# Taking a row's 32nd largest score as the eighth of one MAX8, one pipeline step later

## The chip, the cores and the metric

The kernel runs on one core of a Trainium2 chip. The metric is the device time of one execution in microseconds (us): 872.44 us as the median of three runs of the kernel before (871.95 to 874.28).

The engines are called by the profile's names: PE (TensorE matmuls), PEld (its weight loads), DVE (VectorE), ACT (ScalarE), POOL (GpSimd) and SP (SyncE, which here only issues DMAs).

## The reference

For 4 batches, 8 heads, 576 tokens and 64 channels a head, the program computes a sparse attention, a gated convolution block and a mixing block behind it. Only the attention's top-k is touched here:

```python
scores = scale * np.matmul(q, k.transpose(0, 1, 3, 2))
kth = np.partition(scores, -top_k, axis=-1)[..., -top_k:-top_k + 1]   # top_k = 32
mask = scores >= kth
scores = np.where(mask, scores, -1000000000.0)
scores = scores - np.max(scores, axis=-1, keepdims=True)
attn = np.exp(scores)
attn = attn / (np.sum(attn, axis=-1, keepdims=True) + 1e-09)
```

The attention's output goes through the gated block (`_moe_ref`) and the mixing block (`_moe2_ref`), which are matrix products with 512x512 and 576x576 weights.

## The kernel before, in words

The scores come as 144 tiles of 128 rows by 576 columns. The main loop runs over pipeline steps; in step i each stage works on another tile, and the list `STEP` (for the first 72 steps `SOON`) sets the order of the stages within a step. The orders of DVE and ACT are exactly the order in which the program is written (`FIXED`); PE, POOL and SP are ordered by a planner, by priorities that follow the written order and by when it expects inputs to be ready.

A tile j passes these stages:

- Step j, `pick`: six MAX8 (L573), each over 96 columns, leave 48 candidates a row.
- Step j+1, still `pick`: three MAX8 (L577) and two MATCH_REPLACE8 (L579) over the 48 candidates give the row's 24 largest candidates, `tops`; the 24th is the bound t.
- Step j+1, `count` (ACT, L585): n is the sign of t against each score, +1 where the score is below t and -1 elsewhere, and its sum over the row goes to `acc`. So `acc` = 576 - 2c, where c is how many scores are not below t. c is 24 unless one block of 96 columns held more than eight of the row's largest.
- Step j+2, `below` (POOL, L593): y = score times n, so all scores at or above t become negative.
- Step j+3, `rest` (DVE, L598): MAX8 over y gives the eight largest scores below t. The tile y has a single buffer, so `below` of the next tile waits for this MAX8.
- Once for each group of three tiles, `select` puts three DVE operations into the list `apart`: L611 compares `acc` with eight constants (`counts`), L613 multiplies the outcome by the eight values, L614 adds them up. What is left is the one value that is the row's 32nd, in `thrs`. `mask_between` issues them one at a time around the mask of a step: L611 before the mask, L613 and L614 behind it, each behind an operation of the weights' conversion if there is one.
- Step j+5, `expo` (ACT), and step j+6, `mask` (DVE, L656): the score is compared with the threshold and multiplied by the exponential, in place.

Behind these stand the transposes, the products with v, the convolution, and as `jobs` the matmuls of the two blocks, of which each step takes a portion by planned cost. GpSimd also does subtractions that split numbers into a high and a low part (L244 for heads, L403 for matrices), the convolution's first sum (L796), joins converted weights (L342), negates maxima (L603), and prepares sums (L700).

`check` looks once, behind the last tile, whether any threshold is not to be trusted; then the whole work would be done again in a slower way (`safe`), which the inputs here don't need.

Of the kernel before, what the change touches and what calls it, by code (L numbers as in the profile page):

```python
# [92 lines left out]
def mixer(ctx, tc, qT, kT, vt, w_val, conv_t, w_out, w_theta, w_tok, w_ch, out, flag):  # L93
    nc = tc.nc
    safe = flag is None
    P = 128
    B, S, DM = vt.shape
# [5 lines left out]
    G = 3  # L103
    NSUB = 6
    SUB = S // NSUB
    K = 32
    KC = 24
# [3 lines left out]
    CUT = 2 * P  # L111
    COLS = ((0, CUT), (CUT, S))
    LAG = G + FLAG

    cp = ctx.enter_context(tc.tile_pool(name="cp", bufs=1))
    io = ctx.enter_context(tc.tile_pool(name="io", bufs=1))
    sp = ctx.enter_context(tc.tile_pool(name="sp", bufs=1))
    wk = ctx.enter_context(tc.tile_pool(name="wk", bufs=1))
# [34 lines left out]
    N = len(seq)  # L153
# [10 lines left out]
    make_identity(nc, ident)  # L164
    ones = cp.tile([P, 1], F32, name="ones")
    nc.gpsimd.memset(ones, 1.0)
    counts = cp.tile([P, G, K - KC], F32, name="counts")
    for i in range(K - KC):
        nc.gpsimd.memset(counts[:, :, i : i + 1], S - 2.0 * (K - 1 - i))
    trig_bias = cp.tile([P, 1], F32, name="trig_bias")  # L170
    nc.gpsimd.memset(trig_bias[:64], math.pi / 2)
    nc.gpsimd.memset(trig_bias[64:], 0.0)
# [3 lines left out]
    nc.gpsimd.memset(magic, MAGIC)  # L176

    awake = cp.tile([P, 1], F32, name="awake")
    said = cp.tile([1, 2], F32, name="said")
    thrs = cp.tile([P, N], F32, name="thrs")  # L180
    least = cp.tile([P, N, 2], F32, name="least")
    taken, lacking = set(), {}
    raws, heads, there, ready = {}, {}, set(), set()
    s_tiles, s_psum, groups, xT, gate, W, ms = {}, {}, {}, {}, {}, {}, {}
    owed = [0.0]
    jobs, later, mid, extras, chains, flowing, fill, apart = [], [], [], [], [], [], [], []

    evicted = [None]
    last = {}

    def tabled(out, src, func, **more):

        ins = nc.scalar.activation(out, src, func, **more).ins  # L193
        table = func == AF.Sin
        if (not table) in last and TABLED:
            tc.add_manual_dep(ins, last[not table].name, mybir.DependencyInfo(
                mybir.DependencyClass.NoSync, mybir.DependencyReason.DATA), reason="one table at a time")
        last[table] = ins

    def run(fs):  # L200
        for f in fs:
            f()
# [342 lines left out]
    def scores_out(i):  # L545
        banks = s_psum.pop(i)
        if i < N:
            st = sp.tile([P, S], F32, tag="s", name=f"s_{i}", bufs=LAG + TO + AHEAD)
            for (lo, hi), (bank, _) in zip(COLS, banks):
                evicted[0] = nc.scalar.activation(st[:, lo:hi], bank[:, : hi - lo], AF.Copy, scale=0.125).ins  # L550
            s_tiles[i] = st
        for _, follow in banks:
            run(follow)

    def group(i):
        g, k = divmod(i, G)
        if g not in groups:
            d = {}
            for nm, shape in (("cand", [P, G, 8 * NSUB]), ("tops", [P, G, K]), ("acc", [P, G]),
                              ("eq", [P, G, K - KC])):  # L560
# [20 lines left out]
    def count(i):  # L581

        d, k = group(i)
        n = wk.tile([P, S], BF16, tag="n", name=f"n_{i}")
        nc.scalar.activation(n, s_tiles[i], AF.Sign, bias=d["tops"][:, k, KC - 1 : KC], scale=-(1.0 + 2.0 ** -22),  # L585
                             accum_out=d["acc"][:, k : k + 1])
        d["n", k] = n

    def below(i):

        d, k = group(i)
        y = wk.tile([P, S], F32, tag="y", name=f"y_{i}")
        nc.gpsimd.tensor_tensor(y, s_tiles[i], d.pop(("n", k)), ALU.mult)  # L593
        d["y", k] = y

    def rest(i):
        d, k = group(i)
        nc.vector.max(d["tops"][:, k, KC:K], d.pop(("y", k)))  # L598

    def nmax(g):  # L600

        d = groups[g]
        nc.gpsimd.tensor_scalar(least[:, g * G : g * G + G, :], d["tops"][:, :, 0 : KC : KC - 1], -1.0, None, ALU.mult)  # L603

    def select(g):

        if safe:
            return one_by_one(g)
        d = groups[g]
        tops, acc = d["tops"], d["acc"]  # L610
        apart.append(lambda: nc.vector.tensor_tensor(  # L611
            d["eq"], counts, acc.unsqueeze(2).broadcast_to([P, G, K - KC]), ALU.is_equal))
        apart.append(lambda: nc.vector.tensor_tensor(d["eq"], d["eq"], tops[:, :, KC:], ALU.mult))  # L613
        apart.append(lambda: nc.vector.tensor_reduce(thrs[:, g * G : g * G + G], d["eq"], mybir.AxisListType.X, ALU.add))  # L614

    def one_by_one(g):

        d = groups[g]
        spare = wk.tile([P, S], F32, tag="ct", name=f"spare_{g}")
        for k in range(G):  # L620
            src = s_tiles[g * G + k]
            for r in range(K // 8):
# [5 lines left out]
            nc.vector.tensor_copy(thrs[:, g * G + k : g * G + k + 1], d["tops"][:, k, K - 1 : K])  # L628
        nmax(g)

    def check():

        bad = cp.tile([P, 2], F32, name="bad")
        worse = wk.tile([P, S], F32, tag="ct", name="worse")[:, :N]
        nc.vector.tensor_scalar(worse, thrs, 2.0 ** -100, None, ALU.is_le)
        nc.vector.tensor_reduce(bad[:, 0:1], worse, mybir.AxisListType.X, ALU.add)
        nc.vector.tensor_scalar(worse, least[:, :, 1], -2.0 ** -100, None, ALU.is_ge)
        nc.vector.tensor_reduce(bad[:, 1:2], worse, mybir.AxisListType.X, ALU.add)

        def on_pe(spare):  # L640
            nc.tensor.matmul(spare[:1, :2], ones, bad, start=True, stop=True)
            return lambda: nc.scalar.activation(said, spare[:1, :2], AF.Copy, accum_out=flag)
        extras.append((2, on_pe))

    def expo(i):
        e = seq[i]
        e.exp = wk.tile([P, S], F32, tag="e", name=f"e_{i}", bufs=2)
        tabled(e.exp, s_tiles[i], AF.Exp, bias=least[:, i, 0:1], scale=1.0)

    def mask(i):  # L650
        e = seq[i]
        part = e.part
        if e is part["tiles"][0]:
            part["sums"] = wk.tile([P, 5], F32, tag="sums", name=f"sums_{e.u}_{e.x}", bufs=3)
        p = s_tiles[i]
        nc.vector.scalar_tensor_tensor(p, p, thrs[:, i : i + 1], e.exp, ALU.is_ge, ALU.mult,  # L656
                                       accum_out=part["sums"][:, e.slot : e.slot + 1])

    def turn(i):
# [559 lines left out]
    for k, part in enumerate(order):  # L1219
# [27 lines left out]
    def mask_between(i):  # L1247

        for x in range(3):
            for fs in (fill, apart):  # L1250
                if fs:
                    fs.pop(0)()
            if x == 0:
                inside(i, mask)

# [10 lines left out]
    def inside(i, f):  # L1266
        if 0 <= i < N:
            f(i)
# [18 lines left out]
    def by_group(i, f):  # L1287
        if i % G == 0:
            inside(i, lambda i: f(i // G))
# [4 lines left out]
    def work_1(i):  # L1294
# [3 lines left out]
    DO = {  # L1298
        "count": lambda i: None if safe else inside(i - 1, count),
        "expo": lambda i: inside(i - LAG + 1, expo),  # L1300
        "select": lambda i: by_group(i - G - 2, select),
        "nmax": lambda i: None if safe else by_group(i - G - 1, nmax),
        "check": lambda i: None if safe or i != N + G else check(),
        "mask": lambda i: mask_between(i - LAG),
# [2 lines left out]
        "chains": lambda i: follow_up(),  # L1307
        "convert": convert,
        "pick": lambda i: i <= N and (by_group(i, group_of) if safe else pick(i)),
        "below": lambda i: None if safe else inside(i - 2, below),  # L1310
        "scores_out": lambda i: i + AHEAD - 1 in s_psum and scores_out(i + AHEAD - 1),
        "turn_out": lambda i: inside(i - LAG - TO - 1, turn_out),
        "rest": lambda i: None if safe else inside(i - 3, rest),
        "later": lambda i: run_later(),
        "turn": lambda i: inside(i - LAG - TO, turn),
        "work_1": work_1,
# [60 lines left out]
```

## Time and profile before

| | |
|---|---|
| median of three runs | 872.44 us |
| the profiled execution | 878.3 us |
| its span, first to last instruction | 876.5 us |
| mean granted TensorE clock | 0.932 |
| DVE busy | 725.9 us, 83% of the span |
| PE busy | 757.3 us, 86% |
| ACT busy | 652.3 us, 74% |
| POOL busy | 409.2 us, 47% |

The busy time of an engine is the union of its instructions, so two that overlap in the pipeline count once. A line such as "L613 DVE ... x48 | 16.9, 353 | 0.0" tells the line of the program, the engine, the operation, what it writes and reads, how often, the busy microseconds, the mean nanoseconds of one, and the idle time of the engine before them with what ended it. In a timeline the first number is the start, the second the duration, and brackets hold idle time before it.

### The profile page before, as it was taken

Reading aid. Unit: us, or ns where it says so; the run is one execution under the profiler, and the core shown is the slowest. Engines: PE = TensorE matmul, PEld = TensorE weight load, DVE = VectorE, ACT = ScalarE, POOL = GpSimd, SP = SyncE. Lnnn points to the kernel's source line nnn. Section 1 sums busy time; section 2 is a strip of 40 time slices with the busy share of each in tenths; the row PEclk is TensorE's granted clock in tenths of the full one; section 3 lists DMA queues with packets and bytes.
Section 4 is the critical chain, followed back from the end, with each engine's and each line's share of the span. In section 5 each row is a group of like instructions: output and inputs, shape, how many; then the busy total and the mean of one; then the engine's idle time right before and its main releaser. Section 6 shows DMA issues by size and latency. Waiting matters only on the chain.

```text
span 876.5 us, 15920 instructions
## 1 busy us (share of the span) xinstructions
PE 757.3 (86%) x4526; PEld 575.6 (66%) x4526; DVE 725.9 (83%) x2952; ACT 652.3 (74%) x1591; POOL 409.2 (47%) x435
## 2 busy tenths in 40 slices
PE   4477876947879689989798999999998999999995
PEld 2344554624556358676678577769697776699895
DVE  5999998879999778989999999899988697444522
ACT  5787896878979587687878898798987895445611
POOL 4655555344555324354758634445677233003700
PEclk9996788966899979999899999999999999999998
DMA  5665555613433124324735552132755110042001
GB/s 148 169 183 166 143 141 152 174 48 92 131 92 93 43 67 128 94 55 114 225 112 185 191 163 61 46 94 58 216 135 154 44 67 15 1 155 93 3 1 58
DMA packets 73601, 94.35 MB, mean 108 GB/s; under 512 B 13728, under 2 KB 37152, under 8 KB 73504
## 3 DMA queue, kind: packets, MB, share of 16 engines
q1 hardware_dynamic: 73184, 92.82, 37.6%
q8 instruction: 38, 0.62, 0.3%
q14 instruction: 59, 0.48, 0.2%
q10 hardware_dynamic: 320, 0.43, 0.1%
HBM read 49.96 MB, written 13.11 MB: 72 GB/s over the span
## 4 chain that ended last, share of the span: by engine, by line
PE 41%; DVE 37%; ACT 11%; issue 5%; DMA 2%; POOL 2%; SPq 1%; ACTq 0%; POOLq 0%; DVEq 0%
PE py L1090 8%; DVE cand L573 8%; PE px L749 8%; DVE tops L598 6%; DVE s L656 5%; PE ph L507 4%; PE pval L507 3%; DVE cand L579 3%; PE pt L669 3%; PE py L1109 3%; DVE tops L577 3%; PE px2t L507 3%; DVE gp L804 3%; PE ps L536 2%; PE pth L507 2%
## 5 line engine op out<-in xcount | busy, mean ns | idle before, releaser
L593 POOL TENSOR_TENSOR y<-s,n 128x576 f32<-128x576 f32 x144 | 188.4, 1308 | 199.5 <-DVE tops L598 101.6
L573 DVE MAX8 cand<-s 128x8 f32<-128x96 f32 x864 | 210.8, 245 | 1.4 <-ACT s L550 1.4
L585 ACT ACTIVATE n<-s,tops 128x576 bf16<-128x576 f32 x144 | 112.0, 778 | 50.3 <-DVE tops L577 34.4
L656 DVE SCALAR_TENSOR_TENSOR s<-s,thrs,e 128x576 f32<-128x576 f32 x144 | 137.9, 958 | 5.7 <-ACT e L193 5.7
L669 PE MATMUL pt<-ident,s 128*128 128x128 f32 x576 | 99.0, 296 | 49.3 <-ACT pT L688 34.5
L550 ACT ACTIVATE s<-ps 128x256 f32<-128x256 f32 (+1 forms) x288 | 103.9, 406 | 38.2 <-PE ps L722 15.0
L669 PEld LDWEIGHTS pt<-ident,s 128*128 128x128 f32 x576 | 71.1, 149 | 78.1 <-ACT pT L688 42.6
L1090 PE MATMUL py<-w_tok,z 128*128 128x256 f32 (+1 forms) x432 | 115.6, 410 | 6.9 <-DVE z L949 6.7
L749 PE MATMUL px<-pT,v 128*64 128x256 f32 (+3 forms) x640 | 113.3, 455 | 8.2 <-ACT pT L688 7.2
L598 DVE MAX8 tops<-y 128x8 f32<-128x576 f32 x144 | 108.0, 750 | 11.7 <-POOL y L593 11.7
L193 ACT ACTIVATE e<-s,least 128x576 f32<-128x576 f32 x144 | 110.5, 768 | 1.3 <-DVE s L656 0.9
L536 PE MATMUL ps<-kh_None,q 128*128 128x256 f32 x240 | 96.9, 410 | 5.9 <-ACT rb L729 2.7
L688 ACT COPY pT<-pt 128x512 f32<-128x512 f32 x128 | 73.2, 571 | 29.1 <-PE px L749 14.7
L1090 PEld LDWEIGHTS py<-w_tok,z 128*128 128x128 f32 x432 | 78.4, 191 | 24.8 <-issue 7.3
L749 PEld LDWEIGHTS px<-pT,v 128*64 128x64 f32 (+1 forms) x640 | 46.1, 148 | 58.8 <-issue 30.9
L577 DVE MAX8 tops<-cand 128x8 f32<-128x48 f32 x432 | 82.9, 192 | 0.1
L537 PE MATMUL ps<-kl_None,q 128*128 128x256 f32 x240 | 73.7, 309 | 0.0
L536 PEld LDWEIGHTS ps<-kh_None,q 128*128 128x128 f32 x240 | 48.5, 202 | 26.9 <-ACT s L550 7.5
L536 PE MATMUL ps<-kh,q 128*128 128x256 f32 (+1 forms) x80 | 40.1, 506 | 20.5 <-ACT s L550 11.4
L579 DVE MATCH_REPLACE8 cand<-tops,cand 128x48 f32<-128x48 f32 x288 | 55.3, 192 | 0.0
L804 DVE SCALAR_TENSOR_TENSOR gp<-xT,w_conv,gp 128x576 f32<-128x576 f32 (+2 forms) x60 | 50.1, 836 | 4.7 <-POOL gp L796 4.0
L537 PEld LDWEIGHTS ps<-kl_None,q 128*128 128x128 f32 x240 | 49.1, 205 | 3.4 <-issue 1.6
(208 smaller groups left out, 1695.7 us busy)
## 6 DMA issues: line engine op xcount, KB each, us to landing
kh_None<-kh_None SPq DMA_DIRECT2D x48, 144.0 KB, 2.5
kl_None<-kl_None SPq DMA_DIRECT2D x48, 144.0 KB, 2.6
v<-in_vt_dram SPq DMA_DIRECT2D x20, 256.0 KB, 2.9
out_dram<-x2T SPq DMA_DIRECT2D x16, 256.0 KB, 3.2
w<-ch SPq DMA_DIRECT2D x16, 256.0 KB, 4.3
w<-theta SPq DMA_DIRECT2D x16, 256.0 KB, 5.5
raw_hi<-in_w_tok_dram SPq DMA_DIRECT2D x14, 256.0 KB, 2.9
kh<-kh SPq DMA_DIRECT2D x24, 144.0 KB, 2.4
```

Of the source, the lines that this page charges most:

```text
L193: ins = nc.scalar.activation(out, src, func, **more).ins
L536: nc.tensor.matmul(bank[:, :w], q2, kh[:, lo:hi], start=(j == js[0]), stop=False)
L537: nc.tensor.matmul(bank[:, :w], q2, kl[:, lo:hi], start=False, stop=(j == js[-1]))
L573: nc.vector.max(d["cand"][:, k, 8 * x : 8 * x + 8], s_tiles[i][:, x * SUB : (x + 1) * SUB])
L577: nc.vector.max(top, c)
L585: nc.scalar.activation(n, s_tiles[i], AF.Sign, bias=d["tops"][:, k, KC - 1 : KC], scale=-(1.0 + 2.0 ** -22), accum_out=d["acc"][:, k : k + 1])
L593: nc.gpsimd.tensor_tensor(y, s_tiles[i], d.pop(("n", k)), ALU.mult)
L598: nc.vector.max(d["tops"][:, k, KC:K], d.pop(("y", k)))
L656: nc.vector.scalar_tensor_tensor(p, p, thrs[:, i : i + 1], e.exp, ALU.is_ge, ALU.mult, accum_out=part["sums"][:, e.slot : e.slot + 1])
L669: nc.tensor.transpose(e.pt[:, c, :], p[:, c * P : (c + 1) * P], ident)
L749: nc.tensor.matmul(px[64 * j : 64 * j + 64, :], v[r, c, 64 * j : 64 * j + 64], pT[r, k, :], start=(c == 0), stop=(c == NF), skip_group_che ...
L1090: nc.tensor.matmul(ps, z[:, m * P : (m + 1) * P], W["tok"][:, w, lo:hi], start=(i + k == 0), stop=(i == NF))
```

## The change

The columns of y grow from 576 to 584 (`NK` = 8). POOL fills the eight new ones with `steps` - `acc`, where `steps` holds 576 - 2(24 + i) - 1, so that the column i holds 2(c - 24 - i) - 1: at least 1 for i below c - 24, negative otherwise. Scores are scaled by a further 2^-30 when they leave PSUM (`SMALL`, undone in the scale of the exponential and of the negated maxima), so each of these positive numbers is above every score. The MAX8 over all 584 columns then holds c - 24 of them and behind them the 32 - c largest scores below t: its eighth is the row's 32nd largest score. It is written to `thrs` in a backward order, so that the eighth value stays and the other seven are written over by later tiles.

The three operations of `select`, the list `apart`, `counts` and `eq` go. `below` and `rest` run for tile i-3 and i-4 in step i in place of i-2 and i-3, and n has two buffers. `check` tests one bound more (two DVE operations).

```diff
-    counts = cp.tile([P, G, K - KC], F32, name="counts")
-    for i in range(K - KC):
-        nc.gpsimd.memset(counts[:, :, i : i + 1], S - 2.0 * (K - 1 - i))
+    steps = cp.tile([P, NK], F32, name="steps")
+    for i in range(NK):
+        nc.gpsimd.memset(steps[:, i : i + 1], S - 2.0 * (KC + i) - 1.0)
...
-                evicted[0] = nc.scalar.activation(st[:, lo:hi], bank[:, : hi - lo], AF.Copy, scale=0.125).ins
+                evicted[0] = nc.scalar.activation(st[:, lo:hi], bank[:, : hi - lo], AF.Copy, scale=0.125 * SMALL).ins
...
-        n = wk.tile([P, S], BF16, tag="n", name=f"n_{i}")
+        n = wk.tile([P, S], BF16, tag="n", name=f"n_{i}", bufs=2)
...
-        y = wk.tile([P, S], F32, tag="y", name=f"y_{i}")
-        nc.gpsimd.tensor_tensor(y, s_tiles[i], d.pop(("n", k)), ALU.mult)
+        y = wk.tile([P, S + NK], F32, tag="y", name=f"y_{i}")
+        nc.gpsimd.tensor_tensor(y[:, :S], s_tiles[i], d.pop(("n", k)), ALU.mult)
+        nc.gpsimd.tensor_tensor(y[:, S:], steps, d["acc"][:, k : k + 1].broadcast_to([P, NK]), ALU.subtract)
...
-        nc.vector.max(d["tops"][:, k, KC:K], d.pop(("y", k)))
+        nc.vector.max(thrs[:, N - 1 - i : N - 1 - i + NK], d.pop(("y", k)))
...
-        apart.append(lambda: nc.vector.tensor_tensor(
-            d["eq"], counts, acc.unsqueeze(2).broadcast_to([P, G, K - KC]), ALU.is_equal))
-        apart.append(lambda: nc.vector.tensor_tensor(d["eq"], d["eq"], tops[:, :, KC:], ALU.mult))
-        apart.append(lambda: nc.vector.tensor_reduce(thrs[:, g * G : g * G + G], d["eq"], mybir.AxisListType.X, ALU.add))
...
-        nc.vector.scalar_tensor_tensor(p, p, thrs[:, i : i + 1], e.exp, ALU.is_ge, ALU.mult,
+        nc.vector.scalar_tensor_tensor(p, p, thr(i), e.exp, ALU.is_ge, ALU.mult,
...
-        "below": lambda i: None if safe else inside(i - 2, below),
+        "below": lambda i: None if safe else inside(i - 3, below),
...
-        "rest": lambda i: None if safe else inside(i - 3, rest),
+        "rest": lambda i: None if safe else inside(i - 4, rest),
```

DVE's order has 4231 rows in the program before and 4089 now (both with the safe way, which isn't run), POOL's 708 and 851. The order of ACT is the same throughout, and that of PE and SP but for some places where neighbours change.

DVE in step 83, from the last MAX8 of `pick` to the `rest` of the next step (`s_77` and the other numbers behind a name are tiles, `lo3` and `hi3` parts of a weight, `xT` an output of the attention), before:

```order
L573 MAX cand_27_5046<-s_83_5073 128x8
L611 TENSOR_TENSOR eq_26_4826<-counts_98,acc_26_4825 128x24
L656 SCALAR_TENSOR_TENSOR s_77_4637,sums_8_0_4838<-s_77_4637,thrs_116,e_77_5135 128x576
L613 TENSOR_TENSOR eq_26_4826<-eq_26_4826,tops_26_4824 128x24
L614 TENSOR_REDUCE thrs_116<-eq_26_4826 128x3
L767 TENSOR_TENSOR xT_7_4818<-px_7_1_4960,rb_7_1_4845 128x320
L403 TENSOR_TENSOR lo3_0_5153<-w_val_127,hi3_0_5152 128x512
L598 MAX tops_27_5047<-y_81_5187 128x8
```

and now:

```order
L574 MAX cand_27_5017<-s_83_5043 128x8
L653 SCALAR_TENSOR_TENSOR s_77_4609,sums_8_0_4809<-s_77_4609,thrs_116,e_77_5106 128x576
L764 TENSOR_TENSOR xT_7_4789<-px_7_1_4932,rb_7_1_4816 128x320
L405 TENSOR_TENSOR lo3_0_5124<-w_val_127,hi3_0_5123 128x512
L600 MAX thrs_116<-y_80_5158 128x8
```

The three operations around the mask are gone, and the MAX8 at the head of step 84 takes tile 80 in place of tile 81.

POOL at the same place, from the product y of tile 80, before:

```order
L593 TENSOR_TENSOR y_80_5120<-s_80_4854,n_80_5087 128x576
L244 TENSOR_TENSOR kl_10_None_5115<-kl_10_None_5115,kh_10_None_5182 128x576
L593 TENSOR_TENSOR y_81_5187<-s_81_4928,n_81_5159 128x576
L244 TENSOR_TENSOR ql_10_None_5117<-ql_10_None_5117,qh_10_None_5184 128x576
L403 TENSOR_TENSOR X_1_0_4938<-xT_7_4818,X_1_0_4938 128x256
L593 TENSOR_TENSOR y_82_5245<-s_82_5001,n_82_5228 128x576
L603 TENSOR_SCALAR least_117<-tops_27_5047 128x6
L700 TENSOR_SCALAR rs_8_0_5354<-sums_8_0_4838 128x4
L796 TENSOR_TENSOR gp_7_5209<-gp_7_5209,ct_7_1_1_5266 128x576
```

and now:

```order
L594 TENSOR_TENSOR y_80_5158<-s_80_4825,n_80_5057 128x576
L595 TENSOR_TENSOR y_80_5158<-steps_98,acc_26_4797 128x8
L246 TENSOR_TENSOR ql_10_None_5087<-ql_10_None_5087,qh_10_None_5155 128x576
L405 TENSOR_TENSOR X_1_0_4910<-xT_7_4789,X_1_0_4910 128x256
L594 TENSOR_TENSOR y_81_5214<-s_81_4900,n_81_5130 128x576
L595 TENSOR_TENSOR y_81_5214<-steps_98,acc_27_5019 128x8
L609 TENSOR_SCALAR least_117<-tops_27_5018 128x6
L697 TENSOR_SCALAR rs_8_0_5324<-sums_8_0_4809 128x4
L594 TENSOR_TENSOR y_82_5300<-s_82_4971,n_82_5197 128x576
L793 TENSOR_TENSOR gp_7_5178<-gp_7_5178,ct_7_1_1_5235 128x576
L595 TENSOR_TENSOR y_82_5300<-steps_98,acc_27_5019 128x8
```

Each product y is followed by the small subtraction for the eight columns, and the products stand one step further back against the other work. At tile 82 the planner has put the convolution's sum (`gp`, which waits for ACT's `ct`) between the two; such a pair is parted at 9 of the 144 tiles.

## Rows read from the trace of the kernel before

**Rows 1.** The page: the chain that ended last, shares of the span by engine.

```profile
PE 41%; DVE 37%; ACT 11%; issue 5%; DMA 2%; POOL 2%; SPq 1%; ACTq 0%; POOLq 0%; DVEq 0%
```

**Rows 2.** Busy by stretch: start:end, length, engines' busy us (instructions), clock, DMA.

```profile
20.00:740.00 720.00, 622.06 (x3628) 455.96 (x3629) 661.04 (x2794) 588.24 (x1456) 372.59 (x380) 0.92 0.42 117
380.00:400.00 20.00, 16.14 (x110) 13.26 (x111) 19.89 (x70) 16.84 (x39) 9.46 (x10) 0.96 0.33 75
```

**Rows 3.** Groups of instructions on DVE.

```profile
L573 DVE MAX8 cand<-s 128x8 f32<-128x96 f32 x864 | 210.8, 245 | 1.4 <-ACT s L550 1.4
L656 DVE SCALAR_TENSOR_TENSOR s<-s,thrs,e 128x576 f32<-128x576 f32 x144 | 137.9, 958 | 5.7 <-ACT e L193 5.7
...
L613 DVE TENSOR_TENSOR eq<-eq,tops 128x24 f32<-128x24 f32 x48 | 16.9, 353 | 0.0
L611 DVE TENSOR_TENSOR eq<-counts,acc 128x24 f32<-128x24 f32 x48 | 16.9, 351 | 0.0
```

**Rows 4.** Timeline of DVE around one undisturbed select, at 37 us.

```profile
37.09 0.18 DVE L611 TENSOR_TENSOR eq<-counts,acc 128x24 f32<-128x24 f32 x1
37.18 0.81 DVE L656 SCALAR_TENSOR_TENSOR s<-s,thrs,e 128x576 f32<-128x576 f32 x1
...
38.12 0.18 DVE L613 TENSOR_TENSOR eq<-eq,tops 128x24 f32<-128x24 f32 x1
38.24 0.43 DVE L324 SCALAR_TENSOR_TENSOR raw_lo<-raw_lo,tmp 128x256 int32<-128x256 int32 x1
38.59 0.17 DVE L614 TENSOR_REDUCE thrs<-eq 128x3 f32<-128x24 f32 x1
38.67 0.75 DVE L598 MAX8 tops<-y 128x8 f32<-128x576 f32 x1
```

**Rows 5.** Timeline of POOL and DVE, steps 83 and 84, from 423.9 us.

```profile
423.97 1.27 POOL L593 TENSOR_TENSOR y<-s,n 128x576 f32<-128x576 f32 x1
...
424.19 1.10 DVE L611 TENSOR_TENSOR eq<-counts,acc 128x24 f32<-128x24 f32 x1
...
425.20 1.40 POOL L244 TENSOR_TENSOR ql_None<-ql_None,qh_None 128x576 fp32r<-128x576 f32 x1
...
425.21 2.01 DVE L656 SCALAR_TENSOR_TENSOR s<-s,thrs,e 128x576 f32<-128x576 f32 x1
...
426.56 1.24 POOL L403 TENSOR_TENSOR X<-xT,X 128x256 fp32r<-128x256 f32 x1
...
427.15 0.69 DVE L613 TENSOR_TENSOR eq<-eq,tops 128x24 f32<-128x24 f32 x1
```

**Rows 6.** Who waited for whom: total us, times, longest us.

```profile
POOL y L593 <- ACT n L585: 41.5, 15, 10.0
...
DVE tops L598 <- POOL y L593: 11.7, 9, 2.4
```

**Rows 7.** Timeline of DVE and POOL at the start: the first two MAX8 over y.

```profile
16.00 0.76 DVE L598 MAX8 tops<-y 128x8 f32<-128x576 f32 x1 [2.42 <-POOL y L593]
...
16.85 1.41 POOL L292 TENSOR_TENSOR kl<-raw,kh 128x576 fp32r<-128x576 f32 x1
...
19.52 0.76 DVE L598 MAX8 tops<-y 128x8 f32<-128x576 f32 x1 [1.12 <-POOL y L593]
```

**Rows 8.** Timeline of POOL and DVE at 532 us: a late product.

```profile
532.58 1.50 POOL L593 TENSOR_TENSOR y<-s,n 128x576 f32<-128x576 f32 x1 [0.86 <-ACT n L585]
...
532.86 1.82 DVE L804 SCALAR_TENSOR_TENSOR gp<-xT,w_conv,gp 128x576 f32<-128x576 f32 x1
```

**Rows 9.** Timeline of POOL and DVE from 329 us: an early product.

```profile
329.61 1.29 POOL L593 TENSOR_TENSOR y<-s,n 128x576 f32<-128x576 f32 x1 [2.71 <-DVE tops L598]
...
332.99 0.75 DVE L598 MAX8 tops<-y 128x8 f32<-128x576 f32 x1
```

**Rows 10.** Groups of instructions on POOL: the two nearest to the added subtraction.

```profile
L603 POOL TENSOR_SCALAR least<-tops 128x6 f32<-128x6 f32 x48 | 30.0, 624 | 9.6 <-DVE tops L577 5.2
...
L342 POOL TENSOR_TENSOR w_conv<-raw_hi 128x20 int32<-128x20 int32 x1 | 0.2, 218 | 0.8 <-DVE raw_hi L324 0.8
```

More of the change, by code (lines that the diff above doesn't have):

```diff
@@ L113, in mixer @@
     LAG = G + FLAG
+    NK = K - KC
+    SMALL = 1.0 if safe else 2.0 ** -30
     cp = ctx.enter_context(tc.tile_pool(name="cp", bufs=1))
@@ L178, in mixer @@
     awake = cp.tile([P, 1], F32, name="awake")
-    said = cp.tile([1, 2], F32, name="said")
-    thrs = cp.tile([P, N], F32, name="thrs")
+    said = cp.tile([1, 3], F32, name="said")
+    thrs = cp.tile([P, N + NK - 1], F32, name="thrs")
     least = cp.tile([P, N, 2], F32, name="least")
@@ L185, in mixer @@
     owed = [0.0]
-    jobs, later, mid, extras, chains, flowing, fill, apart = [], [], [], [], [], [], [], []
+    jobs, later, mid, extras, chains, flowing, fill = [], [], [], [], [], [], []
     evicted = [None]
@@ L558, in group @@
             d = {}
-            for nm, shape in (("cand", [P, G, 8 * NSUB]), ("tops", [P, G, K]), ("acc", [P, G]),
-                              ("eq", [P, G, K - KC])):
+            for nm, shape in (("cand", [P, G, 8 * NSUB]), ("tops", [P, G, K if safe else KC]), ("acc", [P, G])):
                 d[nm] = wk.tile(shape, F32, tag=nm, name=f"{nm}_{g}", bufs=2 if nm == "cand" else 3)
@@ L597, in rest, with thr @@
         d, k = group(i)
-        nc.vector.max(d["tops"][:, k, KC:K], d.pop(("y", k)))
+        nc.vector.max(thrs[:, N - 1 - i : N - 1 - i + NK], d.pop(("y", k)))
+    def thr(i):
+        at = N - 1 - i + NK - 1
+        return thrs[:, at : at + 1]
     def nmax(g):
         d = groups[g]
[L603 to L610, printed above, removed]
-        apart.append(lambda: nc.vector.tensor_tensor(
-            d["eq"], counts, acc.unsqueeze(2).broadcast_to([P, G, K - KC]), ALU.is_equal))
-        apart.append(lambda: nc.vector.tensor_tensor(d["eq"], d["eq"], tops[:, :, KC:], ALU.mult))
-        apart.append(lambda: nc.vector.tensor_reduce(thrs[:, g * G : g * G + G], d["eq"], mybir.AxisListType.X, ALU.add))
+        nc.gpsimd.tensor_scalar(least[:, g * G : g * G + G, :], d["tops"][:, :, 0 : KC : KC - 1], -1.0 / SMALL, None,
+                                ALU.mult)
     def one_by_one(g):
@@ L627, in one_by_one @@
                     src = spare
-            nc.vector.tensor_copy(thrs[:, g * G + k : g * G + k + 1], d["tops"][:, k, K - 1 : K])
+            nc.vector.tensor_copy(thr(g * G + k), d["tops"][:, k, K - 1 : K])
         nmax(g)
     def check():
-        bad = cp.tile([P, 2], F32, name="bad")
+        bad = cp.tile([P, 3], F32, name="bad")
         worse = wk.tile([P, S], F32, tag="ct", name="worse")[:, :N]
[L635 to L638, printed above, removed]
+        for j, (what, limit, op) in enumerate(((thrs[:, NK - 1 :], 2.0 ** -90, ALU.is_le),
+                                               (thrs[:, NK - 1 :], 0.5, ALU.is_ge),
+                                               (least[:, :, 1], -2.0 ** -60, ALU.is_ge))):
+            nc.vector.tensor_scalar(worse, what, limit, None, op)
+            nc.vector.tensor_reduce(bad[:, j : j + 1], worse, mybir.AxisListType.X, ALU.add)
         def on_pe(spare):
-            nc.tensor.matmul(spare[:1, :2], ones, bad, start=True, stop=True)
-            return lambda: nc.scalar.activation(said, spare[:1, :2], AF.Copy, accum_out=flag)
-        extras.append((2, on_pe))
+            nc.tensor.matmul(spare[:1, :3], ones, bad, start=True, stop=True)
+            return lambda: nc.scalar.activation(said, spare[:1, :3], AF.Copy, accum_out=flag)
+        extras.append((3, on_pe))
     def expo(i):
@@ L647, in expo @@
         e.exp = wk.tile([P, S], F32, tag="e", name=f"e_{i}", bufs=2)
-        tabled(e.exp, s_tiles[i], AF.Exp, bias=least[:, i, 0:1], scale=1.0)
+        tabled(e.exp, s_tiles[i], AF.Exp, bias=least[:, i, 0:1], scale=1.0 / SMALL)
     def mask(i):
@@ L1249, in mask_between @@
         for x in range(3):
-            for fs in (fill, apart):
-                if fs:
-                    fs.pop(0)()
+            if fill:
+                fill.pop(0)()
             if x == 0:
@@ L1300, in mixer @@
         "expo": lambda i: inside(i - LAG + 1, expo),
-        "select": lambda i: by_group(i - G - 2, select),
+        "select": lambda i: by_group(i - G - 2, one_by_one) if safe else None,
         "nmax": lambda i: None if safe else by_group(i - G - 1, nmax),
```

## The prediction, made before the changed kernel was run

> **What bounds the kernel now.** Read the page's chain first: it runs 41% over PE and 37% over DVE [rows 1]. So no single engine bounds the kernel; the stretches take turns. The windows show where: from 20 to 740 us, while the 144 tiles pass, DVE is busy for 661 of 720 us, and in the stretch from 380 to 400 us for 19.89 of 20 with PE at 16.14 [rows 2]. Behind 740 us PE alone works through the last blocks, and this change touches nothing there. One tile takes 720 / 144 = 5.0 us.
>
> The chain's 37% are 0.37 x 876.5 = 324 us of DVE. Nearly all lie before 740 us, so a microsecond taken from DVE at a random place there lies on the chain with a chance of 324 / 740 = 0.44. That factor is used below.
>
> **What the change takes from DVE.** The groups say that L611 and L613 take 351 and 353 ns in the mean [rows 3]. The undisturbed ones take 0.18 us each, and they overlap with their neighbours: from the start of L611 to the start of the mask are 0.09 us, from L613 to the next operation 0.12, from L614 to the next 0.08 [rows 4]. The three slots are 0.29 us for each group of three tiles, and 48 x 0.29 = 13.9 us in all. **First term: 13.9 us.**
>
> The rest of their busy time is waiting inside the instruction. The timeline at 424 us shows for what [rows 5]: L611 starts at 424.19, 0.22 us into a product y on POOL, and ends at 425.29, just as that product does (423.97 + 1.27 = 425.24). L613 starts at 427.15 during POOL's L403 and ends with it at 427.8. A DVE operation with two operands in SBUF stands still until POOL's operation is over. For L613 this costs 48 x (353 - 180) = 8.3 us. Behind it stand L614, which goes too, and often operations that need not wait, such as L767, whose first operand lies in PSUM (the order of step 83). I credit 7 of the 8.3; the ends are 0 and 8.3. **Second term: 7 us.**
>
> L611's waits, 48 x (351 - 180) = 8.2 us, would be met by the mask behind it, so they count as nothing. But there is a second loss [rows 5]: when the product ended, L611 got its turn, and POOL's next operation began at 425.20, ahead of the mask, which then took 2.01 us against 0.81 undisturbed [rows 4]. Over 144 masks such waits are 144 x (958 - 810) = 21.3 us [rows 3]. L611 stands ahead of one mask in three: I credit a third. The ends are 0 and 21.3. **Third term: 7 us.**
>
> **What the later step brings.** DVE waited for y 11.7 us in 9 waits [rows 6]. Two of them are at the start, 2.42 and 1.12 us [rows 7]; the second product stood behind a splitting of heads, L292, that ran on POOL until 18.26, and DVE could have gone on with the next tile. I credit 3 us, and they are on the path whole, since nothing else runs then. Of the other 8.2 us I credit half: POOL waited for n from ACT 15 times [rows 6], and n is now ready a step earlier; the other half are products behind other work of POOL, which stay. **Fourth term: 4 us, and 3 at the start.**
>
> A late product also holds DVE up where DVE doesn't wait for it. At 532.58 a product began after 0.86 us of waiting for n; L804 began at 532.86 and took 1.82 us [rows 8], where the mask, the same operation on the same shape, takes 0.81 [rows 4]. That is 1.0 us lost. Had n been there, the product would have run while DVE does MAX8 after MAX8, which have one operand and don't stand still. If half of the 15 late products meet such an operation, it is 7.5 us; the ends are 0 and 15. **Fifth term: 7.5 us.** The Trainium skill says the same in general (SBUF — State Buffer, "Who interferes with whom"): a VectorE instruction with two SBUF inputs contends with a GpSimd instruction that reads SBUF, one with a single input does not. By that rule the two places above are no accident; the trace agrees with its 1.10 us for L611 against 0.18.
>
> **What it adds.** The MAX8 over y grows by eight columns. From 96 to 576 columns a MAX8 goes from 245 to 750 ns [rows 3, 4], 1.05 ns a column: 144 x 8.4 ns = **1.2 us**. `check` adds two short operations behind the last tile, where PE sets the end: nothing, or about 0.5 us if they were exposed. The second buffer of n and the changed scales add no instruction, and ACT's order is the same.
>
> The subtraction on POOL, 128x8, is not in the trace. The nearest rows are a two-operand operation of 128x20 with 218 ns and a strided one of 128x6 with 624 ns, waits included [rows 10]: 31 to 90 us more on POOL. I take the first, which is the nearer in kind. Its cover: POOL is busy for 373 of 720 us [rows 2], and an early product ends long before its MAX8, at 330.90 for one that starts at 332.99 [rows 9], 2.1 us of room for 0.22. It costs DVE nothing then. Where the product is late, DVE can stand still 0.22 us longer: 15 times 0.22, **3.3 us**. The ends are 0 and 90.
>
> **The sum.** On DVE: 13.9 + 7 + 7 + 4 + 7.5 - 1.2 - 3.3 = 34.9 us, about 5% of the 661. On the chain: 0.44 x 34.9 = 15.3, with the start 18.3. Where DVE is relieved another engine is next: PE leaves 3.9 us of room from 380 to 400 us, but over all 720 us only 98, or 2.7 for each 20 us, and unevenly [rows 2]. I let two thirds through, which is a choice: 12 us. Against the profiled execution's own 878.3 us that is 866; that execution lies 5.9 us above the median of the runs, and against the median 872.4 it is **860 us**.
>
> A difference of 0.3% (2.6 us) is about what a measurement of this kernel can tell from no change.
>
> **The rivals.**
>
> *More than that.* If products now always start right behind the MAX8, most of the masks' 21.3 us of standing still go, and the 18.3 us come through whole: 0.44 x 14 = 6 us more, 24 in all, 848 to 855 us. For it: an early product needed nothing but the MAX8 [rows 9]. Against it: at the start it was POOL's own L292 that made a product late [rows 7], and such work stays. Chance 0.16.
>
> *The later step brings nothing.* If lateness is POOL's queue and not n, the fourth and fifth terms fall away: 23.4 x 0.44 + 3 = 13, two thirds of it 9; with less let through, 864 to 870 us. For it: only 15 of 144 products waited for n at all. Chance 0.16.
>
> *Hidden.* PE or ACT set the step in most places and only the start's 3 us or less are seen: 870 to 875 us. For it: 41% of the chain is PE. Against it: DVE's 661 of 720 us, more than PE's 622 [rows 2]. Chance 0.11.
>
> *Slower: the added subtraction.* It is 144 more operations of POOL that make DVE's two-operand work stand still, and at 9 tiles the convolution's sum parts it from its product, so that the MAX8 waits for that too. It decides if each costs DVE more than the gain of 34.9 + 3.3 and the start's 3, 41 us / 144 = 0.29 us a tile. At the 0.62 us of L603 it would be 89 us; (89 - 41) x 0.44 = 21, two thirds of it 14: 875 to 886 us. The Trainium skill warns of this (Perfetto Trace Analysis, "Optimizing Scalar/DVE Operations"): the two engines share an SBUF read port, so handing work from one to the other might not help. Against it: 2.1 us of room [rows 9]. Chance 0.09.
>
> **How the numbers follow.** The forecast, 855 to 864 us, has 0.48. Faster by over 0.3% are the forecast and the first two rivals: 0.80. The same: 0.11. Slower: 0.09. The range 849 to 871 us takes in the forecast, the second rival, most of the first and the edge of the third, which leaves out about 2 in 10.
>
> **What would show it.** DVE's busy time falls from 726 to about 690 us, with no L611, L613 or L614; the MAX8 over y takes about 758 ns; the mask's mean falls from 958 towards 900 ns; the waits of POOL's y for ACT's n shrink to a few microseconds; DVE's first two waits go; POOL's busy time grows by some 31 us. It is wrong if the masks' mean rises, if MAX8 waits for the subtraction in more than a few tiles, or if DVE's time falls as said and the span does not.

## The result and the profile after

The changed kernel takes **863.82 us** in the median of four runs (863.16 to 864.24), beside 873.29 us (871.95 to 874.28) for the kernel before. The ratio is 0.9892, with a 95% interval from 0.9874 to 0.991: 9.5 us faster. The profiled execution of the kernel before lay some 5 us above its median, so the two spans, 876.5 and 862.1 us, differ by more than the kernels do. Below, times are compared by medians and ratios, and the traces are used to see where time is spent.

The page of the changed kernel: busy time of each engine, and the chain that ended last by engine.

```profile
PE 752.4 (87%) x4526; PEld 574.1 (67%) x4526; DVE 696.0 (81%) x2810; ACT 650.4 (75%) x1591; POOL 441.4 (51%) x579
...
PE 47%; DVE 24%; ACT 16%; issue 5%; POOL 5%; DMA 2%; SPq 0%; ACTq 0%; POOLq 0%; DVEq 0%
```

DVE fell from 725.9 to 696.0 us and from 37% of the chain to 24%; PE rose from 41% to 47%, ACT from 11% to 16% [rows 1]. The same by windows (columns as in [rows 2]):

```profile
20.00:740.00 720.00, 629.79 (x3683) 463.35 (x3684) 636.39 (x2658) 590.29 (x1462) 406.25 (x525) 0.92 0.43 117
380.00:400.00 20.00, 18.37 (x136) 14.95 (x135) 19.96 (x80) 17.90 (x45) 9.20 (x11) 1.00 0.41 96
```

From 380 to 400 us DVE is as full as before, 19.96 of 20 us, but PE works 18.37 us there where it worked 16.14 [rows 2]. Groups that answer to [rows 3] and [rows 10]:

```profile
L653 DVE SCALAR_TENSOR_TENSOR s<-s,thrs,e 128x576 f32<-128x576 f32 x144 | 141.9, 985 | 5.7 <-ACT e L195 5.7
L600 DVE MAX8 thrs<-y 128x8 f32<-128x584 f32 x144 | 109.2, 759 | 5.7 <-POOL y L595 5.5
...
L594 POOL TENSOR_TENSOR y<-s,n 128x576 f32<-128x576 f32 x144 | 188.3, 1307 | 192.4 <-DVE thrs L600 153.7 <-ACT e L195 10.8 <-DVE cand L574 9.1
L595 POOL TENSOR_TENSOR y<-steps,acc 128x8 f32<-128x8 f32 x144 | 38.2, 266 | 0.0
```

The MAX8 over 584 columns takes 759 ns; the masks (now L653) take 985 ns in the mean, **more** than the 958 before. The list of waits, as in [rows 6]:

```profile
POOL y L594 <- DVE thrs L600: 153.7, 74, 9.8
ACT n L586 <- POOL y L595: 29.6, 22, 3.0
...
DVE thrs L600 <- POOL y L595: 5.5, 5, 2.0
...
POOL y L594 <- ACT n L586: 2.3, 2, 1.9
```

The product's wait for n went from 41.5 to 2.3 us and DVE's wait for y from 11.7 to 5.5. There is a new wait: n on ACT waits 22 times, 29.6 us in all, for the subtraction on POOL. A likely reason is that n writes its count into a column of the same `acc` tile that the subtraction reads. It takes the place of another: n waited for `tops` 30 times, 34.4 us in all, in the kernel before, and 7 times, 5.2 us, now.

At the start (compare [rows 7]) the first wait fell from 2.42 to 0.40 us and the second, behind L292, is gone:

```profile
16.09 0.77 DVE L600 MAX8 thrs<-y 128x8 f32<-128x584 f32 x1 [0.40 <-POOL y L595]
```

### The profile page after: what moved, and what is told of

Read it like the earlier page. It is cut to its first block, busy times and chain, and to the rows that moved or that the text cites. A ratio compares the mean times of both kernels' runs of the same rounds, so it can differ in the third digit from the quotient of the medians.

```text
span 862.1 us, 15907 instructions
## 1 busy us (share of the span) xinstructions
PE 752.4 (87%) x4526; PEld 574.1 (67%) x4526; DVE 696.0 (81%) x2810; ACT 650.4 (75%) x1591; POOL 441.4 (51%) x579
## 4 chain that ended last, share of the span: by engine, by line
PE 47%; DVE 24%; ACT 16%; issue 5%; POOL 5%; DMA 2%; SPq 0%; ACTq 0%; POOLq 0%; DVEq 0%
PE py L1087 10%; PE px L746 9%; DVE cand L574 5%; PE ph L509 5%; DVE thrs L600 4%; PE pt L666 4%; PE ps L538 3%; PE px2t L509 3%; PE py L1106 3%; PE pth L509 3%; PE pval L509 3%; DVE s L653 2%; PE ps L539 2%; ACT n L586 2%; DVE cand L580 2%
## 5 line engine op out<-in xcount | busy, mean ns | idle before, releaser
L653 DVE SCALAR_TENSOR_TENSOR s<-s,thrs,e 128x576 f32<-128x576 f32 x144 | 141.9, 985 | 5.7 <-ACT e L195 5.7
L586 ACT ACTIVATE n<-s,tops 128x576 bf16<-128x576 f32 x144 | 112.1, 779 | 41.1 <-POOL y L595 29.6
L746 PE MATMUL px<-pT,v 128*64 128x256 f32 (+3 forms) x640 | 109.3, 440 | 8.3 <-ACT pT L685 8.0
L600 DVE MAX8 thrs<-y 128x8 f32<-128x584 f32 x144 | 109.2, 759 | 5.7 <-POOL y L595 5.5
L746 PEld LDWEIGHTS px<-pT,v 128*64 128x64 f32 (+1 forms) x640 | 44.0, 142 | 57.2 <-issue 26.2
L801 DVE SCALAR_TENSOR_TENSOR gp<-xT,w_conv,gp 128x576 f32<-128x576 f32 (+2 forms) x60 | 45.7, 761 | 6.1 <-POOL gp L793 5.4
```

Of the source, the lines that this page charges most:

```text
L600: nc.vector.max(thrs[:, N - 1 - i : N - 1 - i + NK], d.pop(("y", k)))
L653: nc.vector.scalar_tensor_tensor(p, p, thr(i), e.exp, ALU.is_ge, ALU.mult, accum_out=part["sums"][:, e.slot : e.slot + 1])
L746: nc.tensor.matmul(px[64 * j : 64 * j + 64, :], v[r, c, 64 * j : 64 * j + 64], pT[r, k, :], start=(c == 0), stop=(c == NF), skip_group_che ...
```

## The experiments

Each ratio is against the kernel before on the same chip, in five rounds, with its 95% interval. "Steps" are those of `below` and `rest` (i-3 and i-4 in the changed kernel, i-2 and i-3 before).

**1. The threshold alone: trick_only.** The changed kernel with the old steps.

```diff
-        "below": lambda i: None if safe else inside(i - 3, below),
+        "below": lambda i: None if safe else inside(i - 2, below),
...
-        "rest": lambda i: None if safe else inside(i - 4, rest),
+        "rest": lambda i: None if safe else inside(i - 3, rest),
```

> The changed kernel with the product and its MAX8 back at their old steps (i-2 and i-3): the threshold from one MAX8 alone. Theory A (the three DVE operations that go are what shortens the kernel): 864 to 867 us, at least two thirds of the 9.5 us that the whole change gained. Theory B (the later step, by freeing the product from ACT's n, brings a third or more): 867 to 872 us, and POOL's products wait for n for some 40 us as in the kernel before. By my own sum the later step was worth 8 of 18 us.

Measured: 864.3 us, ratio 0.9908 [0.9884, 0.9932]. Its list of waits:

```profile
POOL y L594 <- ACT n L586: 36.1, 11, 9.4
...
DVE thrs L600 <- POOL y L595: 17.3, 13, 2.6
```

The waits that the later step was to end are there, and on DVE three times the 5.5 us; the time is that of the full change within the intervals, as theory A has it. So the later step gives nothing by itself that these runs can tell, and the threshold gives the gain.

**2. The later step alone: shift_only.** The kernel before with the later steps. The select had to go a step later too, with its three operations issued together, and n has the second buffer.

```diff
-        "select": lambda i: by_group(i - G - 2, select),
+        "select": lambda i: by_group(i - G - 3, select),
...
-        "below": lambda i: None if safe else inside(i - 2, below),
+        "below": lambda i: None if safe else inside(i - 3, below),
...
-        "rest": lambda i: None if safe else inside(i - 3, rest),
+        "rest": lambda i: None if safe else inside(i - 4, rest),
```

> The kernel before with the product and its MAX8 one step later and a second buffer of n; select comes one step later as well and issues its three operations together ahead of the first mask that needs them. Theory A: 871 to 875 us, no difference that can be told. Theory B: 864 to 870 us. If the waits of the products for n go from 41.5 us to a few and the time stays, lateness for n was off the path.

Measured: 879.04 us, ratio 1.0073 [1.0048, 1.0099]: slower, which neither theory had, although no wait of the products for n is in the list and DVE's waits for y are down to 2.6 us. Since the select moved as well, it doesn't settle what the step alone is worth in the kernel before.

**3. The operations put back: back_two, back_one, back_six.** The changed kernel, with operations that compute nothing for the output put where the select's stood. back_two: a comparison and a product with two operands and 128x24 elements, and a sum. back_one: three sums with one operand in each group of three tiles, one at each of the three places around the mask. back_six: six, two at each place. The edit shown is back_one's.

```diff
+    def idle(g):
+        for x in range(3):
+            apart.append(lambda: nc.vector.tensor_reduce(spent[:, g * G : g * G + G], counts, mybir.AxisListType.X, ALU.add))
...
-        "select": lambda i: by_group(i - G - 2, one_by_one) if safe else None,
+        "select": lambda i: by_group(i - G - 2, one_by_one if safe else idle),
```

> The changed kernel with three idle operations put back on DVE at the old places for each group of three tiles: the same two comparisons and products with two operands in SBUF and the sum, into tiles that nobody reads. Theory A: the gain goes, 870 to 875 us. Theory B: 864 to 868 us. The operations' busy time should be about 42 us again, of which 25 are their own.

> As the run with three idle operations put back, but each has a single operand (three sums over 24 columns), so that none should stand still behind POOL. If the slots of the three operations are what counted (13.9 of my sum), it takes back more than half of the gain: 868 to 872 us. If the waits inside them and behind them counted more (14 of my sum, and the slots hidden), 864 to 867 us.

> The changed kernel with six idle one-operand sums over 24 columns for each group of three tiles, twice as many as in the run with three of them: some 26 us on DVE, about as much as the three two-operand operations held it busy, but spread evenly and without a wait for POOL. Theory G (DVE came off the path by some 13 us, and what it gets back beyond that counts, whatever it is spent on): 868 to 875 us, near the 873.6 us of the run with the two-operand operations. Theory F (it is the waits in single pieces of over 1 us that count): 863 to 867 us.

Measured: back_two 873.63 us, ratio 0.9996 [0.9975, 1.0016]; back_one 863.39, 0.9887 [0.9865, 0.9909]; back_six 882.5, 1.0107 [1.0081, 1.0134]. The groups of back_two:

```profile
L614 DVE TENSOR_TENSOR eq<-eq,counts 128x24 f32<-128x24 f32 x48 | 18.2, 379 | 0.0
L612 DVE TENSOR_TENSOR eq<-counts,acc 128x24 f32<-128x24 f32 x48 | 16.7, 347 | 0.0
...
L615 DVE TENSOR_REDUCE spent<-eq 128x3 f32<-128x24 f32 x48 | 8.4, 176 | 1.0
```

and of back_one, with DVE's total:

```profile
PE 751.4 (87%) x4526; PEld 571.4 (66%) x4526; DVE 709.2 (82%) x2954; ACT 651.5 (75%) x1591; POOL 441.3 (51%) x580
...
L612 DVE TENSOR_REDUCE spent<-counts 128x3 f32<-128x24 f32 x144 | 24.5, 170 | 1.0
```

and of back_six:

```profile
PE 758.8 (86%) x4526; PEld 575.6 (65%) x4526; DVE 731.8 (83%) x3098; ACT 653.0 (74%) x1591; POOL 442.4 (50%) x580
...
L612 DVE TENSOR_REDUCE spent<-counts 128x3 f32<-128x24 f32 x288 | 50.1, 174 | 6.0
```

Three operations with the old shapes take the whole gain back, as theory A has it. Read with back_one alone, which lies just under the second of its two ranges, this says that standing still in two-operand operations is what costs. back_six takes away that this is all: its operations have one operand and hardly stand still (174 ns in the mean), and it is the slowest of all, far above theory F and 7.5 us above the range of theory G. From the changed kernel to back_one 144 sums add 13.2 us to DVE and nothing to the time; 144 more add 22.6 us to DVE and 19 us to the time.

**4. One operation at a time: back_second and back_first.** back_second puts back only the product behind the mask, back_first only the comparison ahead of it (`apart` then holds it and two empty places). The edit shown is back_second's.

```diff
+        apart.append(lambda: None)
+        apart.append(lambda: nc.vector.tensor_tensor(d["eq"], counts, counts, ALU.mult))
+        apart.append(lambda: None)
```

> The changed kernel with only the second of the three idle operations put back, behind the mask: one product of two constant 128x24 tiles for each group of three tiles. Theory D (it is this operation's standing still behind POOL that costs, since nothing that follows it on DVE needs to wait): at least half of the 9.5 us come back, 868 to 873 us, with 7 to 10 us of waits inside the operation. Theory E (it is the first one, which lets POOL in ahead of the mask): 863 to 866 us.

> The changed kernel with only the first of the three idle operations put back, ahead of the mask: one comparison of constants with acc, two operands in SBUF. Theory D: 863 to 866 us, since the mask would have stood still for the same work of POOL. Theory E: 868 to 873 us, and the mask's mean rises above the 985 ns of the changed kernel.

Measured: back_second 863.87 us, 0.991 [0.9889, 0.9931]; back_first 867.47, 0.994 [0.9923, 0.9957]. The group of back_second, and then those of back_first:

```profile
L612 DVE TENSOR_TENSOR eq<-counts 128x24 f32<-128x24 f32 x48 | 16.7, 348 | 0.0
```

```profile
L663 DVE SCALAR_TENSOR_TENSOR s<-s,thrs,e 128x576 f32<-128x576 f32 x144 | 136.1, 945 | 5.7 <-ACT e L197 5.7
...
L611 DVE TENSOR_TENSOR eq<-counts,acc 128x24 f32<-128x24 f32 x48 | 15.0, 313 | 0.0
```

The product behind the mask stands still 48 x (348 - 180) = 8 us and costs nothing that can be told, against theory D. The comparison stands still less, the masks behind it are 40 ns shorter than in the changed kernel, and DVE's total is only 700.6 us; still the kernel is 3.6 us slower, between the ranges of the two theories, and theory E's sign, longer masks, is not there. That is not explained by DVE's busy time and stays open.

**5. The old kernel with operations of one operand: before_one.** The kernel before with the select's three operations replaced by three sums; the mask reads the eighth value of the MAX8 directly. Its expectation says what it leaves out.

```diff
-        apart.append(lambda: nc.vector.tensor_tensor(
-            d["eq"], counts, acc.unsqueeze(2).broadcast_to([P, G, K - KC]), ALU.is_equal))
-        apart.append(lambda: nc.vector.tensor_tensor(d["eq"], d["eq"], tops[:, :, KC:], ALU.mult))
-        apart.append(lambda: nc.vector.tensor_reduce(thrs[:, g * G : g * G + G], d["eq"], mybir.AxisListType.X, ALU.add))
+        for x in range(3):
+            apart.append(lambda: nc.vector.tensor_reduce(thrs[:, g * G : g * G + G], counts, mybir.AxisListType.X, ALU.add))
```

> The kernel before with each of the three operations replaced by a sum over 24 columns, which has one operand; the mask takes the eighth value of the MAX8 as it is. This leaves out the correction for rows where c is not 24. Theory F (waits for POOL inside two-operand operations are the whole cost of the select, its slots are hidden): 863 to 867 us, the time of the changed kernel without any of its edits. The rival (the slots count as well, and the run with one-operand idle operations was a lucky order): 867 to 872 us.

Measured: 868.59 us, 0.995 [0.9932, 0.9968], DVE 712.2 us: half of the gain, with as many operations as before, in the range of theory F's rival.

**6. The old steps with room taken away: trick_back_one.** back_one with the old steps, the edit of experiment 1.

> The run with three idle one-operand operations, but the product and its MAX8 at their old steps. Theory I (the later step gives DVE the room in which these operations cost nothing, though alone it gains nothing): 867 to 870 us, as the kernel before with one-operand operations (868.6 us). If the later step is worth nothing even so: 863 to 866 us.

Measured: 867.94 us, 0.9936 [0.9912, 0.996], DVE 713.5 us. Its waits:

```profile
POOL y L597 <- ACT n L589: 38.9, 14, 9.8
...
DVE thrs L603 <- POOL y L598: 14.7, 12, 2.6
```

These are the waits of trick_only, where they cost nothing that can be told. Beside 144 idle sums the kernel with the later step is 867.9 - 863.4 = 4.5 us faster, as theory I has it. The two intervals only just part, and the difference is hardly larger than the 3.6 us of back_first that nothing explains.

**7. The subtraction taken away: no_steps.** y is one fixed tile whose last eight columns hold a constant. Its expectation says what it leaves out.

```diff
-        nc.gpsimd.tensor_tensor(y[:, S:], steps, d["acc"][:, k : k + 1].broadcast_to([P, NK]), ALU.subtract)
```

> The changed kernel without the subtraction on POOL: the eight columns hold -1 throughout. This leaves out the correction for rows where c is not 24. If the 144 subtractions are hidden, 862 to 865 us; if they lengthen the masks' standing still (985 ns in the mean against 958 before), 857 to 861 us.

Measured: 862.45 us, 0.9881 [0.9865, 0.9897]. The 144 subtractions, 38.2 us on POOL and 29.6 us of ACT's waits (3.7 here, where n waits 34.0 us for `tops` again), cost some 1.4 us, which the intervals don't part from nothing: they are hidden. The masks take 975 ns in the mean without them, so most of the rise from 958 to 985 is not theirs.

**8. A second y: y_two and least_one.** y_two gives y two buffers; to make room, POOL negates only the largest score for the mask's exponent and the last test of `check` reads that. least_one has only the second edit.

```diff
-        y = wk.tile([P, S + NK], F32, tag="y", name=f"y_{i}")
+        y = wk.tile([P, S + NK], F32, tag="y", name=f"y_{i}", bufs=2)
```

> The changed kernel with a second buffer for y, so that a product need not wait for the MAX8 of the tile before. To make room, POOL keeps only the largest score of a row and not its 24th, and the check's third test looks at that one. Theory H (late products cost): POOL's waits for the MAX8, 153.7 us, nearly vanish, the masks' mean falls below 958 ns, 857 to 862 us. The rival: the single buffer holds the product back until DVE is at its one-operand operations; without it the masks' mean rises above 985 ns and the time is 864 to 870 us.

> The changed kernel with only what the run with two buffers for y needs to make room: POOL negates three values a group in place of six, and the check's third test looks at the largest score. Off the path: 862 to 865 us.

Measured: y_two 863.55 us, 0.9883 [0.9859, 0.9907]; least_one 864.2, 0.9892 [0.9869, 0.9916]. In y_two DVE's waits for y are all but gone:

```profile
DVE thrs L600 <- POOL y L595: 0.4, 1, 0.4
```

and the time is the same, between the ranges of theory H and its rival. So DVE's last waits for y are off the path. That holds for them alone: the products are late in other ways here, since they wait 55.9 us for n (2.3 in the changed kernel) and still 75.4 us for the MAX8, and while the masks' mean falls to 957 ns, that of the convolution's L801 on 128x576 rises from 880 to 990 ns. No version beat the changed kernel by more than the intervals tell.

## Why the prediction was right

**The size.** Forecast were 12 us out of 34.9 us taken from DVE, and 860 us. Measured are 9.5 us out of 725.9 - 696.0 = 29.9. The time lies 4 us above the forecast and inside its range. The main mechanism, fewer operations on the engine that bounded the middle, was right; several terms, and the way the sum was scaled, were not, and that these errors nearly cancel is luck. Without the third, fourth and fifth terms and the start's 3 us, the prediction's own scaling gives (34.9 - 18.5) x 0.44 x 2/3 = 4.8 us, half of what was measured: credits that brought little made up for a share that was too low.

**What was taken from DVE (first and second terms).** Experiments 1 and 3 show that these operations are the gain: without them the old steps reach 864.3 us, with idle ones of the same shapes the new steps are back at 873.63. But the two terms can't be told apart by adding: 8 us of standing still behind the mask cost nothing in back_second, and the sums' slots alone cost nothing in back_one.

**The masks (third term, 7 us).** This failed, with its sign: the masks' mean rose by 27 ns, 144 x 27 = 3.9 us more, where 7 us less were forecast; a rising mean is one of the signs by which the prediction said it would be wrong. The mean does not go with the time either: it is lowest, 939 ns, in back_two. The other half of the argument held: L611's waits are now met by the mask behind it. back_first shows it the other way round: the comparison, back in its place, stands still 48 x (313 - 180) = 6.4 us, and the masks are 144 x 40 ns = 5.8 us shorter. The mask still meets late products, and standing still goes both ways. At the same place as in [rows 5], step 83, the timeline of the changed kernel shows:

```profile
414.15 1.42 POOL L246 TENSOR_TENSOR kl_None<-kl_None,kh_None 128x576 fp32r<-128x576 f32 x1 [2.29 <-ACT kh_None L240]
...
415.52 1.28 POOL L594 TENSOR_TENSOR y<-s,n 128x576 f32<-128x576 f32 x1
...
415.74 1.68 DVE L653 SCALAR_TENSOR_TENSOR s<-s,thrs,e 128x576 f32<-128x576 f32 x1
...
416.76 0.72 POOL L595 TENSOR_TENSOR y<-steps,acc 128x8 f32<-128x8 f32 x1
...
417.44 1.42 POOL L246 TENSOR_TENSOR ql_None<-ql_None,qh_None 128x576 fp32r<-128x576 f32 x1
```

The product is late behind POOL's own L246; the mask stands still until it is over; then the subtraction, 0.20 us undisturbed, stands still 0.72 us until the mask is over.

**The later step (fourth and fifth terms, 11.5 us, and 3 at the start).** The forecast of the waits came true (41.5 to 2.3 us, 11.7 to 5.5, and the first mask starts 1.9 us earlier than before), but not their worth: experiment 1 has the waits and loses nothing that can be told. The start's 3 us, called on the path whole, did not reach the end: trick_only's first mask starts 1.9 us after the changed kernel's (29.24 and 27.36 us), its last one 1.8 us ahead of it (736.06 and 737.88). So the rival "the later step brings nothing" holds for the change as it was made. That the step gives room for further operations is a reading of the 4.5 us in experiment 6, and not shown beyond it. The fifth term came true on DVE in part: the 36 operations of the convolution on 128x576, L804 of [rows 8] and now L801, took 4.5 us less, where 7.5 were forecast. Before and now:

```profile
L804 DVE SCALAR_TENSOR_TENSOR gp<-xT,w_conv,gp 128x576 f32<-128x576 f32 x36 | 36.2, 1005 | 2.1 <-POOL gp L796 1.6
```

```profile
L801 DVE SCALAR_TENSOR_TENSOR gp<-xT,w_conv,gp 128x576 f32<-128x576 f32 x36 | 31.7, 880 | 3.3 <-POOL gp L793 2.9
```

With the old steps, in trick_only, they take 934 ns in the mean, and the kernel's time is the same.

**What was added.** The MAX8 took 759 ns where 758 were forecast, POOL's time grew by 32.2 us where 31 were, and the subtraction is hidden (experiment 7), close to the forecast, which took 3.3 us of DVE's relief for it, and against the rival "slower".

**The scaling.** The prediction took one even share, 0.44 x 2/3 = 0.29, for every microsecond. The runs look like a bend instead (DVE's busy time is that of the one profiled execution, the median that of all runs):

```
kernel                    DVE busy us    median us
no_steps                  694.4          862.45
changed kernel            696.0          863.82
least_one                 698.0          864.2
trick_only                699.6          864.3
y_two                     700.3          863.55
back_first                700.6          867.47
back_second               701.9          863.87
back_one                  709.2          863.39
before_one                712.2          868.59
trick_back_one            713.5          867.94
back_two                  720.0          873.63
shift_only                722.6          879.04
kernel before             725.9          873.29
back_six                  731.8          882.5
```

Up to 709 us on DVE the time is 862.4 to 864.3 us for seven of eight kernels. Above, it rises, by 19 us for 22.6 from back_one to back_six. Read so, of the 29.9 us the first 17 gave the 9.5 us, more than half each, and the last 13 gave nothing: there the rival "hidden" is true, and the profile's own sign for it (DVE's time falls and the span does not) is back_one beside the changed kernel. DVE's busy time holds standing still as well as work, so it is a guide and no law: back_first and shift_only lie off the curve by 3.6 us and some 5, the kernel before and back_two are 5.9 us apart on DVE and alike in time, and why is open. An edit also shifts other operations in the order, PE's and POOL's among them; that was not held fixed.

The share of 0.44 came from DVE's part of the chain, and the chain does not price DVE here: the slowest kernel, back_six, has less of it on DVE than y_two, which is as fast as the changed kernel. First back_six, then y_two:

```profile
PE 40%; DVE 27%; ACT 17%; POOL 6%; issue 5%; DMA 3%; SPq 1%; ACTq 0%; POOLq 0%
```

```profile
PE 45%; DVE 32%; ACT 11%; issue 5%; DMA 3%; POOL 2%; SPq 1%; ACTq 0%; POOLq 0%; DVEq 0%
```

**Where it shows.** Busy time from 400 to 500 us, first of the kernel before, then of the changed one, then of back_six and back_one:

```profile
400.00:500.00 100.00, 90.51 (x614) 72.94 (x610) 97.51 (x376) 82.88 (x207) 65.36 (x62) 0.94 0.54 165
```

```profile
400.00:500.00 100.00, 92.61 (x613) 73.94 (x611) 92.73 (x371) 85.97 (x215) 71.01 (x83) 0.93 0.58 174
```

```profile
400.00:500.00 100.00, 90.56 (x615) 73.20 (x615) 97.53 (x409) 84.93 (x210) 70.44 (x83) 0.95 0.55 168
```

```profile
400.00:500.00 100.00, 92.62 (x642) 74.51 (x641) 95.30 (x396) 87.03 (x219) 71.73 (x84) 0.98 0.58 180
```

DVE sat at 97.5 of 100 us in the kernel before and does again in back_six; in the changed kernel it is at 92.7, level with PE. But back_one, no slower, has it at 95.3 with PE at 92.6, so relief stopped paying before the two were level, and that PE sets the pace from there on is not shown. The prediction saw that PE is next (98 us of room in 720) but spread that room evenly. Where the gain arises can be seen: the mask of tile 83 starts at 454.35 us before and at 443.23 now, that of the last tile at 750.29 and 737.88, so in these executions nearly all of the gain is there by tile 83.

**A rival for the free 13 us.** back_one does not run level with the changed kernel. By tile 83 its mask is 5.4 us behind (448.67 and 443.23 us); by tile 95 it has won back 3.9, and the last mask is 1.6 behind; its profiled execution took 2.0 us longer in all. The stretch between these two masks, first in the changed kernel, then in back_one:

```profile
443.20:505.20 62.00, 59.45 (x382) 46.26 (x382) 53.88 (x215) 53.75 (x134) 41.78 (x47) 0.94 0.51 160
```

```profile
448.70:506.70 58.00, 55.27 (x370) 42.79 (x369) 55.34 (x226) 51.48 (x129) 42.82 (x47) 1.00 0.51 163
```

In the changed kernel PE stood still there for 2.5 us until DVE's `rs` (L698) was done and worked only 1.96 us from 472 to 476; then its granted clock was 0.50, which is 1.2 GHz:

```profile
472.00:476.00 4.00, 1.96 (x8) 1.40 (x8) 3.96 (x12) 3.96 (x11) 1.89 (x2) 0.67 0.15 55
476.00:480.00 4.00, 4.00 (x10) 2.51 (x8) 4.00 (x14) 3.46 (x7) 1.56 (x3) 0.50 0.43 161
```

In back_one PE waited 1.2 us for its `rs`, and the clock of the stretch is 1.00. So in these executions the idle sums did cost time up to tile 83, and a stretch in which the changed kernel's clock fell made most of it good. How much of the free 13 us is that, and how much is room on DVE, no run separates.

## What to carry to other kernels

Before a relief of one engine is priced, find how far it can come down before it stops paying, and don't take the chain's share for a price; here relief paid more than half while the engine sat at 97 of 100 us from 400 to 500 us, and the last 13 us of it nothing, with the rival above open. Idle operations added in steps, three and then six, bracket that point in two runs, and they help to tell whether an operation costs by its waits or by its time. Compare as well where in the traces the two kernels part: in one stretch back_one won back 3.9 us here. A long list of waits on an engine that is not the bound, like POOL's 41.5 us for n, can be worth nothing.

## What the runs showed of the hardware

A small POOL operation stands still for DVE too. The subtraction takes 192 ns at the least and 731 at the most; the one of step 83 shown above took 0.72 us behind a mask that was already waiting (the source view of L595: minimum, median and maximum in ns):

```profile
L595 POOL TENSOR_TENSOR y<-steps,acc x144: 192/202/731, 15.8 to 728.5; 128x8 f32<-128x8 f32 x144
```

DVE operations with one operand took 170 and 174 ns in the mean of 144 and 288, so they hardly stood still, where those with two operands and as many elements took 313 to 379, or 250 and 262 in shift_only, where they are issued together; yet the 288 short ones of back_six cost more of the kernel's time than the 96 long ones of back_two with their 48 sums.
